# Zero matmuls and full columns in the first stage of a fused Fourier mixer and MLP, an earlier input load, and one weight conversion moved

## The chip, the cores and the metric

The kernel runs on one core of a Trainium2 chip. The metric is device time in microseconds (us) of one execution; lower is better. All kernels here keep the reference's outputs; every run told below was correct. A run is called fast when the chip was in its normal state; all runs here are fast but one, a single execution whose state can't be told (e8), which is marked. Where a profile is read, times count from the first instruction of that execution.

## The reference, cut to what matters

A Fourier filter over 8 images of 3008 x 256, then a two-layer MLP on all 24064 rows. The two weight matrices reach the kernel as 64-bit floats, which it converts itself.

```python
def _attn_ref(x, filt_r, filt_i):
    X = np.fft.rfft(x, axis=1)
    Y = X * (filt_r + 1j * filt_i)[None, :, :]
    return np.fft.irfft(Y, n=x.shape[1], axis=1).astype(np.float32)

def _moe_ref(x, w_in, w_out):        # x: (24064, 256), w_in: (256, 2048), w_out: (2048, 256)
    h = x @ w_in
    g = h * np.clip(h + 3.0, 0.0, 6.0) / 6.0
    return (g @ w_out).astype(np.float32)
```

## The kernel before

The first image has to be transformed before anything can run in the MLP, so the kernel begins with a serial stretch. It loads the first image (`x0_load`), sends it through the first stage of its transform (`a0_unit`, eight units of 8 matmuls each), multiplies by the filter (`f_unit`, VectorE), and transforms back. Then comes the first block of 512 rows in plain form (`plain_up`, `plain_down`), in eight steps, one for each 256 columns of the hidden layer. Meanwhile VectorE converts the weights: 16 pieces, seven VectorE instructions each (an eighth, `w_abs`, is on ScalarE, which the code calls `nc.scalar` and the profile ACT). Piece 2p is needed by `plain_up(p)`, piece 2p+1 by `plain_down(p)`. From the second block on the kernel uses a recursive product with fewer multiplications; that steady part is not touched.

```python
    def a0_unit(j):
        for dh in range(2):
            ps = bank(0)
            for u in range(4):
                nc.tensor.matmul(ps[:, ds(u * P, 4 * KH)], x0[0:64 + NA, j + u, ts(dh, P)],   # 96 columns
                                 st["start"][0:64 + NA, ds(P, 4 * KH)], start=True, stop=True)
            copy(dh and j not in (8, 12), ...)
# ... (cut)
    def plain_up(p):
        st["g", 0, p] = gp.tile([P, 7, 256], FP32, name="g")
        st["h"] = [psU.tile([P, 512], FP32, name=n) for n in ("al", "be")]     # one buffer each
        for i in range(2):
            for d in range(2):
                nc.tensor.matmul(st["h"][i], w_in[p][:, 2 * d + i, :], xb(0, d), start=d == 0, stop=d == 1)
            relu(i)                # ScalarE, L563
            hswish(0, p, i)        # VectorE, L568: frees al, be
# ... (cut)
        ps = psU.tile([P, 512], FP32, name="al")
        for i in range(2):
            nc.tensor.matmul(ps, zero[:, P:2 * P], zero, start=True, stop=True)
        for j, n, bits in (0, 4, 0), (4, 4, 0), (8, 8, 1), (16, 8, 1), (24, 4, 1), (28, 4, 1):
            x0_load(j, n)
            load_bits(bits)        # 64-bit weights of one piece, 512 KB
        # ... (cut)
        for j in range(0, HC, 4):
            a0_unit(j)
            convert(j == 4)        # piece 0
        # ... (cut: the first image's filter and way back)
        x_load(1, 0)               # x of the second image, first part
        load_bits(8)
        for i in 3, 4:
            w_abs(i)
        convert(4)                 # pieces 1 to 4
        # ... (cut)
        for i, s in enumerate((0, 1, 1, 2, 3, 3, 4, 4, 5, 5, 6)):
            at(s, convert_one)     # pieces 5 to 15, in step s of the plain block
        # ... (cut)
        for c in 1, 2:
            at(c, x_load, 1, c)
```

All of SyncE's loads stand in one in-order queue: a load that waits for its buffer holds up those behind it. (In the trace before, the second x load of the second image stands behind loads of weight bits and is not issued until 98.1 us.)

## Time and profile before

| before | |
|---|---|
| median of 3 runs | 2740.15 us (2732.61 to 2745.07) |
| profiled run | 2743.62 us, span 2741.8 us |
| TensorE busy | 99% of the span |
| VectorE busy | 71% |
| where the edited lines run | first 155 us |

The page gives busy time by engine and, in 40 slices of the span, the clock that TensorE was granted. An engine can read as busy and still be slow: at half clock the same matmul is twice as long (in the trace before, 0.213 us for a matmul of 128 columns, 0.108 at full clock). So for TensorE one reads the clock beside the busy time, and the time of one instruction beside both.

I use four marks, all on VectorE: the start of the first product with the filter (L389), the start of the first conversion after the first image's transform (L241), the end of the last hswish of the plain block (L568), and the start of the first sum of the new block (L544). What lies between the marks are the parts of the beginning.

### The profile page before, as it was taken

What the parts mean: (1) busy time and instruction counts of PE and PEld (TensorE: products, weight loads), DVE (VectorE), ACT (ScalarE), POOL (GpSimd) and SP (SyncE); (2) the same over time, 40 slices, a digit from 0 to 9 for tenths busy, and PEclk for the clock granted to TensorE, in tenths of its full rate; (3) what the DMA queues carried; (4) which work ended last, traced back from release to release, by engine and by line L of the source; (5) the groups of instructions that cost most, each with busy time, mean ns of one, the idle gap of its engine ahead of it and who ended that gap; (6) DMA issues with size and microseconds to landing.
All of it is one profiled execution on the core that took longest, in us unless ns stands there. A gap on an engine that the chain in (4) does not pass through costs nothing.

```text
span 2741.8 us, 47083 instructions
## 1 busy us (share of the span) xinstructions
PE 2706.2 (99%) x18100; PEld 2408.9 (88%) x18100; DVE 1955.9 (71%) x3395; ACT 1329.3 (48%) x2662; POOL 423.1 (15%) x622
## 2 busy tenths in 40 slices
PE   8899999999999999999999999999999999999998
PEld 6578888998899988999889998899988999999997
DVE  6868766777567875678756787578775777766665
ACT  3344455445554455444554445544455444544443
POOL 2423321101211012100121001210012100100000
PEclk8999999999999999999999999999999999999999
DMA  8642233221332123321233212332123321100000
GB/s 212 183 134 78 53 89 90 72 58 47 85 90 77 50 50 91 89 69 50 56 89 98 66 42 62 88 97 69 38 58 91 92 72 39 43 23 24 19 9 16
DMA packets 119645, 195.88 MB, mean 71 GB/s; under 512 B 21561, under 2 KB 82681, under 8 KB 119105
## 3 DMA queue, kind: packets, MB, share of 16 engines
q1 hardware_dynamic: 101663, 148.19, 19.1%
q0 software_dynamic: 17152, 44.23, 7.0%
q8 instruction: 143, 2.34, 0.4%
q14 instruction: 81, 0.66, 0.1%
q10 hardware_dynamic: 606, 0.46, 0.1%
HBM read 120.86 MB, written 71.93 MB: 70 GB/s over the span
## 4 chain that ended last, share of the span: by engine, by line
PE 94%; DVE 4%; DMA 1%; issue 1%; SPq 0%; ACT 0%; POOL 0%; POOLq 0%; DVEq 0%
PE po L594 42%; PE al L518 23%; PE be L518 17%; PE psn L472 4%; PE psf L372 3%; PE psf L349 2%; PE psf L419 2%; DVE s L387 1%; DVE g L568 0%; PE po L616 0%; PE po L318 0%; PE po L372 0%; PE al L605 0%; DMA xs<-in_x_dram 0%; DMA w_all<-in_x_dram 0%
## 5 line engine op out<-in xcount | busy, mean ns | idle before, releaser
L594 PEld LDWEIGHTS po<-w_all,g 128*128 128x128 f32 x10304 | 1368.2, 191 | 142.2 <-issue 38.1
L594 PE MATMUL po<-w_all,g 128*128 128x128 f32 x10304 | 1399.4, 276 | 0.8 <-DVE g L568 0.6
L568 DVE SCALAR_TENSOR_TENSOR g<-r,h 128x512 f32<-128x512 f32 x736 | 511.9, 696 | 275.4 <-ACT r L563 263.6
L563 ACT ACTIVATE r<-h,half_c 128x512 f32<-128x512 f32 x736 | 531.2, 722 | 330.6 <-DVE h L544 318.6
L518 PE MATMUL al<-xt,w_all 128*128 128x256 f32 x2208 | 660.4, 381 | 3.9 <-DVE h L549 3.4
L518 PE MATMUL be<-xn,w_all 128*128 128x256 f32 x1472 | 437.8, 379 | 0.0
L544 DVE TENSOR_TENSOR h<-be,s 128x512 f32<-128x512 f32 x368 | 254.1, 691 | 252.1 <-PE be L518 242.1
L518 PEld LDWEIGHTS al<-xt,w_all 128*128 128x128 f32 x2208 | 335.3, 192 | 6.5 <-DVE h L549 4.7
L518 PEld LDWEIGHTS be<-xn,w_all 128*128 128x128 f32 x1472 | 279.7, 190 | 37.9
L558 ACT ACTIVATE h<-al 128x256 f32<-128x256 f32 x368 | 141.3, 384 | 347.3 <-PE al L518 347.3
L549 DVE TENSOR_TENSOR h<-al,s 128x256 f32<-128x256 f32 x368 | 156.3, 425 | 164.0 <-PE al L518 162.6
L576 DVE TENSOR_TENSOR g<-g 128x512 f32<-128x512 f32 x368 | 257.2, 699 | 12.6
L539 ACT ACTIVATE s<-al 128x256 f32<-128x256 f32 x368 | 141.4, 384 | 198.3 <-PE al L518 198.3
L530 ACT ACTIVATE s<-be 128x256 f32<-128x256 f32 x368 | 141.3, 384 | 176.4 <-PE be L518 176.4
L518 PE MATMUL al<-xn,w_all 128*128 128x256 f32 x736 | 219.9, 381 | 0.5 <-ACT h L558 0.5
L518 PE MATMUL be<-xt,w_all 128*128 128x256 f32 x736 | 218.9, 379 | 0.0
L529 ACT ACTIVATE s<-al 128x256 f32<-128x256 f32 x368 | 141.3, 384 | 70.9 <-PE al L518 70.9
L361 POOL DMA_DIRECT2D z_tmp<-t x192 | 111.1, 582 | 414.0 <-ACT t L352 411.5
L575 DVE TENSOR_TENSOR g<-g 128x256 f32<-128x256 f32 x368 | 162.5, 441 | 12.6
L578 DVE TENSOR_TENSOR g<-g 128x256 f32<-128x256 f32 x368 | 161.0, 437 | 12.5
L518 PEld LDWEIGHTS be<-xt,w_all 128*128 128x128 f32 x736 | 139.8, 190 | 18.9
L650 POOL TENSOR_TENSOR o<-p,o 128x256 f32<-128x256 f32 x45 | 32.7, 727 | 793.9 <-ACT t L422 397.7
(138 smaller groups left out, 1917.9 us busy)
## 6 DMA issues: line engine op xcount, KB each, us to landing
g_tmp<-t POOLq DMA_DIRECT2D x96, 256.0 KB, 3.8
t<-g_tmp SPq DMA_DIRECT2D x188, 120.0 KB
t<-z_tmp SPq DMA_DIRECT2D x42, 512.0 KB
z_tmp<-t POOLq DMA_DIRECT2D x192, 96.0 KB, 3.2
out_dram<-o SPq DMA_DIRECT2D x321, 47.0 KB
xs<-in_x_dram SPq DMA_DIRECT2D x112, 128.0 KB
ft<-in_filt_r_dram SPq DMA_DIRECT2D x88, 128.0 KB
ft<-in_filt_i_dram SPq DMA_DIRECT2D x88, 128.0 KB
```

The costliest lines, as they stand in the source:

```text
L518: nc.tensor.matmul(ps, w_in[p][:, w, :], x, start=start, stop=stop, skip_group_check=True)
L529: nc.scalar.activation(out=s[:, 0, :], in_=al, func=AXT.Copy)
L530: nc.scalar.activation(out=s5, in_=be[:, 1, :], func=AXT.Copy)
L539: nc.scalar.activation(out=s[:, 1, :], in_=al, func=AXT.Copy)
L544: nc.vector.tensor_tensor(out=st["h"][0].rearrange("p (a n) -> p a n", a=2), in0=be, in1=s, op=ALU.add)
L549: nc.vector.tensor_tensor(out=st["h"][1][:, 256:512], in0=al, in1=s5, op=ALU.add)
L563: nc.scalar.activation(out=r, in_=st["h"][i], func=AXT.Relu, bias=half_c, scale=1.0 / 6.0)
L568: nc.vector.scalar_tensor_tensor(out=st["g", k, p][:, o:o + 2, :].rearrange("p a n -> p (a n)"), in0=st["r", i], scalar=1.0, in1=st["h"][i ...
L575: v.tensor_tensor(out=g[:, G1, :], in0=g[:, G3, :], in1=g[:, G22, :], op=ALU.add)
L576: v.tensor_tensor(out=g[:, G3:G2 + 1:2, :], in0=g[:, G3:G1 + 1, :], in1=g[:, G11:G11 + 1, :].broadcast_to([P, 2, 256]), op=ALU.subtract)
L578: v.tensor_tensor(out=g[:, G4, :], in0=g[:, G12, :], in1=g[:, G2, :], op=ALU.subtract)
L594: nc.tensor.matmul(st["po", k][bank][:, part, u, :], g[:, a, ts(u, P)], w_out[p][:, w, :], start=(p == 0 and n in OPENS and u == 0), stop= ...
```

## The change

The intent: keep TensorE's clock up while the first image is still arriving, by running matmuls on zeros in the waits and by streaming all 128 columns instead of 96 (the 32 more columns hold zeros and are not read); and shorten the way to the first hswish, by moving one conversion from ahead of the MLP into it and loading a second part of the next image's x earlier.

```diff
-                nc.tensor.matmul(ps[:, ds(u * P, 4 * KH)], x0[...], st["start"][0:64 + NA, ds(P, 4 * KH)],
+                nc.tensor.matmul(ps[:, ts(u, P)], x0[...], st["start"][0:64 + NA, ts(1, P)],
...
-        for i in range(2):
-            nc.tensor.matmul(ps, zero[:, P:2 * P], zero, start=True, stop=True)
+        def keep_warm(n):
+            for i in range(n):
+                nc.tensor.matmul(ps, zero[:, P:2 * P], zero, start=True, stop=True)
+        keep_warm(2)
...
             a0_unit(j)
+            keep_warm({4: 2, 12: 2, 20: 1}.get(j, 0))
...
-        x_load(1, 0)
-        load_bits(8)
-        for i in 3, 4:
-            w_abs(i)
-        convert(4)
+        for c in range(2):
+            x_load(1, c)
+            load_bits(7 + c)
+        w_abs(3)
+        convert(3)
...
-        for i, s in enumerate((0, 1, 1, 2, 3, 3, 4, 4, 5, 5, 6)):
+        for i, s in enumerate((0, 1, 1, 2, 2, 3, 3, 4, 4, 5, 5, 6)):
...
-        for c in 1, 2:
-            at(c, x_load, 1, c)
+        at(2, x_load, 1, 2)
```

(Cut: repeated operands, marked by "[...]".)

More of the change, by code (lines that the diff above doesn't have):

```diff
@@ L317, in a0_unit @@
             for u in range(4):
-                nc.tensor.matmul(ps[:, ds(u * P, 4 * KH)], x0[0:64 + NA, j + u, ts(dh, P)], st["start"][0:64 + NA, ds(P, 4 * KH)],
+                nc.tensor.matmul(ps[:, ts(u, P)], x0[0:64 + NA, j + u, ts(dh, P)], st["start"][0:64 + NA, ts(1, P)],
                                  start=True, stop=True)
```

## The prediction

> **What bounds the kernel now.** I read the page's engine totals first, then the chain that ended last, then windows, waits and the time-ordered listing of the first 160 us, because every edited line runs there.
>
> The page says who owns the whole span:
>
> ```profile
> PE 2706.2 (99%) x18100; PEld 2408.9 (88%) x18100; DVE 1955.9 (71%) x3395; ACT 1329.3 (48%) x2662; POOL 423.1 (15%) x622
> PEclk8999999999999999999999999999999999999999
> ```
>
> TensorE is busy 99% and at full clock, except in the first slice (68.5 us each). The steady part after about 160 us is not touched, and its work is placed by steps, so a shorter beginning moves everything after it by the same amount. The question is how many microseconds the beginning loses and how many come back.
>
> Windows of that beginning (columns: stretch, length, then PE, PEld, DVE, ACT, POOL busy with counts, granted clock, DMA share, GB/s):
>
> ```profile
> 11.39:15.17 3.78, 3.78 (x32) 3.62 (x32) 2.50 (x6) 2.56 (x3) 0.00 (x0) 1.00 1.04 234
> 17.26:29.98 12.72, 12.72 (x65) 12.59 (x65) 2.72 (x4) 3.32 (x4) 1.37 (x3) 0.55 0.91 226
> 34.57:64.20 29.63, 28.27 (x135) 17.06 (x135) 27.59 (x40) 12.53 (x22) 4.75 (x8) 0.98 0.79 225
> 83.95:149.20 65.25, 61.87 (x228) 35.98 (x228) 58.31 (x92) 23.15 (x38) 31.17 (x50) 0.93 0.67 184
> ```
>
> Row one is the third and fourth first-stage unit: 32 matmul instructions in 3.78 us, 0.118 us each. Row two is the last four units, the same work twice over, 0.199 us per instruction, at clock 0.55. "PE busy" hides this: it says 100%. Row three, the transform of the first image, has VectorE (DVE) at 93%, row four, the plain first block, at 89%. So after the first stage VectorE is the engine that sets the pace until about 149 us.
>
> The waits of TensorE in 0 to 160 us:
>
> ```profile
> PE al L605 <- DVE g L568: 7.0, 2, 5.8
> PE po L318 <- DMA w_all<-in_x_dram: 2.4, 2, 2.1
> PE psf L349 <- DMA xs<-in_x_dram: 2.2, 1, 2.2
> ```
>
> and the chain around the last of them, followed by VectorE's own idling there:
>
> ```profile
> 98.60 8.39 DMA xs<-in_x_dram
> 107.13 2.44 PE psf L349 x8
> 109.58 5.94 PE po L616 x16
> 115.51 1.72 PE al L605 x4
> ```
>
> ```profile
> DVE g L568 <- ACT r L563: 3.4, 3, 1.8
> DVE w_all L259 <- ACT s L232: 0.9, 1, 0.9
> ```
>
> Each wait of 2 us or more drops the clock. The granted clock goes to 0.50 from about 18.6 to 35.7, 80 to 86.9 and 107.3 to 114.2 us. The L616 group of 16 takes 5.94 us in the third stretch, 3.47 to 3.72 elsewhere.
>
> **What the Trainium skill says.** "TensorE: Matmul & The Clock Gate", Part 1: the array's clock is gated to half after an idle window and released after a busy one; the window is about 3.4 us and free-running. This trace agrees: the switches are 3.41 us apart or multiples of it. It does not give the threshold; here the window 15.18 to 18.59, PE busy 1.33 of 3.41 us, was enough to lose the clock. More telling, four following windows were "busy" and did not bring it back; the first to do so held the 256-column L372 matmuls.
>
> Same page, Part 2, "LDWEIGHTS": a weight load's time follows the number of weight columns, not the rows. In the trace the 96-column matmuls (0.118 us at full clock, 0.199 at half) are no faster than the 128-column transposes of L330 (8 in 36.08 to 36.62 and before: one each 0.108 us; 0.213 at half). So they are spaced by loading 128 weight columns, and a quarter of each slot streams nothing. My reading (estimate): 96/128 = 75% activity is too little to release the gate; 128 of 128 is enough. And the extra 32 columns cost nothing.
>
> "SBUF — State Buffer", "Who interferes with whom": a VectorE instruction with two SBUF inputs contends with a GpSimd one that reads SBUF. The trace fits: conversions with GpSimd sums beside them take 5.2 to 6.0 us (120.3 to 131.5), others 4.2 to 4.7.
>
> **The change, part by part.**
>
> *Zeros and full columns, first stage.* A zero matmul is two instructions of 512 columns. From transposes of 128 columns at 0.108 us, that is 0.43 us each at full clock, 0.86 us per zero matmul; at half clock the opening ones show 0.855 us per instruction. Unit pairs are 32 instructions at 0.109 = 3.5 us.
> Before: units 0 and 4 end 11.08, wait to 11.39, units 8 and 12 end 15.17, wait to 17.26 for x, then 12.72 us at half clock to 29.98.
> After: 11.1 + 1.7 (two zeros) = 12.8; + 3.5 = 16.3; + 1.7 = 18.0, past the arrival of x at 17.26; + 3.5 = 21.5; + 0.85 = 22.4; + 3.5 = 25.9. The zeros overshoot two waits (1.4 and 0.7 us): the price of the warm clock. Net 4.1 us on the path, since the last units' x, issued right behind and moved at 226 GB/s (750 KB, 3.4 us), is there by about 21 us.
> The first transposes and first L372 group then also run at full clock. Last copy 26.8, half a turn 0.5, ACT copy 0.6, four L372 instructions 0.9: VectorE's first product starts at about 29.0 instead of 34.57. So this part is worth 5.5 us. The first filter tables must be there by 28 us; they are issued 17.4 to 20.4 us and follow that x at the same rate (768 KB, 3.5 us: estimate 24.5). Later groups gain the same, since TensorE's loop (4.67 us per group) and VectorE behind it only shift.
>
> *Three conversions instead of four.* A conversion is seven VectorE instructions, 4.2 to 4.7 us. TensorE's 5.83 us wait for L568 at 83.49 falls to about 1.6 us: relu ends at 78.4 because its buffers wait for L419, ending 77.66, and conversion 3 ends at 78.1 on the old clock. The cold stretch after it disappears. But VectorE is continuous from 54 to 110 us except 0.58 us, so the conversion is moved, not removed: on VectorE's path it is worth nothing or at most 0.6 us.
>
> *x_load(1,1) ahead.* Before, it sits in SyncE's queue behind the loads of bits that wait for conversions 6 and 7, is issued at 98.1 and lands 107.1. Now it is issued at about 70, right behind the load of piece 0, and is there long before step 3. That removes the 2.2 us wait and the half-clock L616 (5.94 - 3.7 = 2.2), and with it what VectorE lost: 0.89 + 1.84 + 1.03 = 3.8 us idle.
>
> Check by VectorE's sum: hswish of step 0 can start 78.5, conversions from 79.85; twelve conversions at the observed times (4.3, 4.4, 4.2, 4.64, 4.63, 4.95, 4.6, 5.6, 5.24, 4.65, 4.67, 4.65 = 56.5) and seven hswish pairs at 1.25 (8.8) give 145.2, against 149.2 before. So 3.9 us, on the old clock, for the last two parts together, of which the x load is nearly all. Total 5.5 + 3.9 = 9.4 us.
>
> **The rivals.**
> 1. The first stage is bounded by DMA: 226 GB/s at 0.91 to 1.08 share from 5 to 50 us, so an earlier TensorE only waits for tables. Against it: no L372 or L389 group waits for a DMA in this trace, and estimated landings leave some 3 us. If it held, the first part would give 2 to 3 us: total 6, time 2734.
> 2. The clock is lost anyway, because the free-running window falls otherwise or zeros do not count. For: the page warns of the phase. Against: the opening zeros took part in the window that released the clock. Then part one turns into a loss of some 1 to 2 us from the zeros at half clock: total 2 to 3, time 2738. With full columns alone it should recover within two windows.
> 3. The plain stage is held by SyncE's in-order queue: z_store, x loads and tables for image 1 are issued back to back from 137.75 to 153, and ACT waits for them at 153.6. The load before them waits for conversion 13, VectorE's, so the queue moves with VectorE; if not, 2 to 4 us vanish: time 2733 to 2735.
> 4. The kernel before is sometimes luckier than this trace: runs of 2732.6 to 2745.1 fit a gap of 2.09 us that sometimes straddles two windows. Then the change helps the median less than the profile.
>
> **Range and chances.** The profiled run took 2743.62 us; minus 9.4 is 2734. The median before is 2740.15; minus 9.4 is 2730.8. I take 2731.5, leaning to the median. Run-to-run spread of before is 12 us, and the gain may lie between 4 and 12 us, so 2725 to 2738. Two per cent is 55 us; all idle and half-clock loss of the beginning together is under 30, so faster by 2% is 1%, slower by 2% 0.5%.
>
> **What would show each step.** First-stage units at about 0.11 us per instruction throughout, ending near 26 us; clock 1.00 from 8 to 60 us; first L389 near 29. No 5.8 us wait of L605 for L568, instead two or more of 1 to 4 us. L349 without a wait for xs; its load issued near 65 us. VectorE busy over 95% through the plain stage; the first L518 near 141 instead of 151 (150.80). I am wrong if L372 or L389 waits for a table, if the clock is 0.50 between 18 and 35, or if the steady part changes at all: that would move more than everything above.

## The result, and the profile after

The changed kernel took 2734.43 us in the median of 4 runs (2733.80 to 2735.95), beside 2741.46 us for the kernel before on the same chip (four runs with the three from above: 2732.61 to 2745.07). The ratio of the two is 0.998, with a 95% interval of 0.9955 to 1.0005, so "same" at the 2%. The interval holds 1. With e5 below, the changed kernel has eight runs of 2733.80 to 2738.80 us, and 31 of the 34 of the kernel before are above 2738.9. Ratios here are the mean time of one kernel's fast runs over that of the other's of the same rounds, so not quite the ratio of the medians. The profiled runs give spans of 2733.2 and 2741.8 us: 8.6 us apart. All outputs are right.

The page's totals and the granted clock of the kernel after:

```profile
PE 2701.7 (99%) x18110; PEld 2401.1 (88%) x18110; DVE 1954.6 (72%) x3395; ACT 1329.9 (49%) x2662; POOL 422.6 (15%) x622
PEclk9999999999999999999999999999999999999999
```

The clock's first digit went from 8 to 9; TensorE has 4.5 us less to do although ten zero instructions were added, because the same matmuls ran at full clock. Windows of the kernel after (same columns as in the prediction: stretch, length, then busy time and counts of PE, PEld, DVE, ACT, POOL, then clock, DMA share, GB/s):

```profile
17.15:25.39 8.24, 8.24 (x67) 7.57 (x66) 3.07 (x4) 3.36 (x4) 1.37 (x3) 1.00 0.88 229
28.68:57.69 29.01, 27.65 (x135) 16.64 (x134) 27.59 (x40) 12.65 (x22) 4.75 (x8) 1.00 0.95 278
73.94:139.35 65.41, 60.38 (x222) 33.53 (x221) 62.13 (x99) 24.18 (x40) 32.74 (x53) 0.95 0.66 184
```

Row one holds the last four units with a zero matmul between them: 8.24 us at clock 1.00, where before they took 12.72 us at 0.55. Row two is the first image's filter stretch, 29.01 us instead of 29.63. Row three is the plain block: VectorE is now busy 95% (62.13 of 65.41), against 89% before.

TensorE's waits for 0 to 160 us have no line for the first image's x (L318) and none for the second image's (L349) any more. A line that names the x load (`xs`) remains, L500's, and has grown from 0.4 to 1.2 us; but L500 reads `t4` and not `xs` in the code, so the name is probably that of another load. The wait for VectorE is still there, in smaller pieces (total, times, longest):

```profile
PE al L605 <- DVE g L568: 6.6, 6, 2.1
```

The last of these pieces shows in the chain that ended last:

```profile
131.89 0.61 DVE g L568
132.54 3.64 PE al L605 x4
136.18 1.72 PE be L605 x4
```

TensorE waited 2.1 us for L568, lost the clock (0.50 from 132.5 to 135.9), and took 3.64 us for what takes 1.72 at full clock. The listing in order of time has the two x loads of the second image on SyncE's queue:

```profile
62.47 1.74 SPq L288 DMA_DIRECT2D xs<-in_x_dram  x4
...
64.84 3.51 SPq L288 DMA_DIRECT2D xs<-in_x_dram  x4
```

The second used to be issued from 98.1 us on. In the marks (us; the last column is the span less the first L544):

| | first L389 | to first L241 | to end of last L568 | to first L544 | first L544 at | rest |
|---|---|---|---|---|---|---|
| before | 34.57 | 29.63 | 84.99 | 5.79 | 154.98 | 2586.9 |
| after | 28.68 | 29.01 | 81.66 | 7.03 | 146.38 | 2586.8 |
| gain | 5.89 | 0.62 | 3.33 | -1.24 | 8.60 | 0.0 |

The rest of the span is the same to 0.1 us. So all of the 8.6 us is in the beginning. VectorE is not without idling in the plain block: the first hswish now waits 1.38 us for its ReLU, as one conversion less stands ahead of it. What the table can't say is which edit earned what.

### The profile page after: what moved, and what is told of

It is laid out like the page before. It is cut to its first block, busy times and chain, and to the rows that moved or that the text cites. A ratio compares the mean times of both kernels' runs of the same rounds, so it can differ in the third digit from the quotient of the medians.

```text
span 2733.2 us, 47101 instructions
## 1 busy us (share of the span) xinstructions
PE 2701.7 (99%) x18110; PEld 2401.1 (88%) x18110; DVE 1954.6 (72%) x3395; ACT 1329.9 (49%) x2662; POOL 422.6 (15%) x622
## 4 chain that ended last, share of the span: by engine, by line
PE 94%; DVE 4%; issue 0%; ACT 0%; DMA 0%; POOL 0%; SPq 0%; POOLq 0%; DVEq 0%
PE po L594 42%; PE al L518 23%; PE be L518 17%; PE psn L472 4%; PE psf L372 2%; PE psf L349 2%; PE psf L419 2%; DVE s L387 1%; DVE g L568 1%; PE po L318 1%; PE po L372 0%; DVE y L243 0%; DVE y L254 0%; DVE g L575 0%; PE al L727 0%
## 5 line engine op out<-in xcount | busy, mean ns | idle before, releaser
L594 PEld LDWEIGHTS po<-w_all,g 128*128 128x128 f32 x10304 | 1368.2, 191 | 142.1 <-issue 38.1
L568 DVE SCALAR_TENSOR_TENSOR g<-r,h 128x512 f32<-128x512 f32 x736 | 511.6, 695 | 275.5 <-ACT r L563 263.9
L518 PE MATMUL al<-xt,w_all 128*128 128x256 f32 x2208 | 660.4, 381 | 3.9 <-DVE h L549 3.4
L518 PE MATMUL be<-xn,w_all 128*128 128x256 f32 x1472 | 437.8, 379 | 0.0
L544 DVE TENSOR_TENSOR h<-be,s 128x512 f32<-128x512 f32 x368 | 254.0, 690 | 253.5 <-PE be L518 242.3
L518 PEld LDWEIGHTS al<-xt,w_all 128*128 128x128 f32 x2208 | 335.3, 192 | 6.5 <-DVE h L549 4.7
L518 PEld LDWEIGHTS be<-xn,w_all 128*128 128x128 f32 x1472 | 279.7, 190 | 38.0
L518 PE MATMUL al<-xn,w_all 128*128 128x256 f32 x736 | 219.9, 381 | 0.5 <-ACT h L558 0.5
L518 PE MATMUL be<-xt,w_all 128*128 128x256 f32 x736 | 218.9, 379 | 0.0
L518 PEld LDWEIGHTS be<-xt,w_all 128*128 128x128 f32 x736 | 139.8, 190 | 18.9
```

Source lines behind the costliest of these rows:

```text
L518: nc.tensor.matmul(ps, w_in[p][:, w, :], x, start=start, stop=stop, skip_group_check=True)
L544: nc.vector.tensor_tensor(out=st["h"][0].rearrange("p (a n) -> p a n", a=2), in0=be, in1=s, op=ALU.add)
L568: nc.vector.scalar_tensor_tensor(out=st["g", k, p][:, o:o + 2, :].rearrange("p a n -> p (a n)"), in0=st["r", i], scalar=1.0, in1=st["h"][i ...
L594: nc.tensor.matmul(st["po", k][bank][:, part, u, :], g[:, a, ts(u, P)], w_out[p][:, w, :], start=(p == 0 and n in OPENS and u == 0), stop= ...
```

## The experiments

The theory to test: zeros and full columns together keep the clock in the first stage (5.9 us), the x load ahead gives the plain block's 3.3 us, and the moved conversion gives nothing. Rivals: one of the two first-stage edits does it all; or the moved conversion is what counts; or what is gained at the front is given back at the waits behind. Twelve runs were made (e5 repeats the changed kernel, e10 repeats e6). Medians of 4 runs (e8: one run; e12: five):

| run | kernel | median (us) | before | first L389 | to L241 | to L568 | to L544 | L544 at | rest |
|---|---|---|---|---|---|---|---|---|---|
| e1 | before + full columns | 2734.65 | 2740.70 | 27.74 | 29.01 | 84.46 | 5.80 | 147.01 | 2586.8 |
| e2 | before + zeros | 2735.30 | 2740.70 | 28.40 | 29.00 | 81.62 | 7.03 | 146.05 | 2586.8 |
| e3 | before + both | 2736.28 | 2740.70 | 29.10 | 29.01 | 82.75 | 5.80 | 146.66 | 2586.8 |
| e4 | before + x load + three conversions | 2740.30 | 2740.70 | 36.59 | 29.83 | 80.94 | 7.03 | 154.39 | 2586.8 |
| e5 | after, again | 2736.49 | 2740.81 | 29.28 | 29.01 | 81.50 | 5.80 | 145.59 | 2586.9 |
| e6 | after without zeros | 2733.07 | 2740.81 | 27.35 | 29.33 | 81.53 | 5.79 | 144.00 | 2587.0 |
| e7 | e6 with four conversions | 2735.85 | 2740.81 | 29.42 | 29.01 | 81.52 | 7.04 | 146.99 | 2586.8 |
| e8 | e1 with x of unit 16 late | 2734.06 | 2740.81 | 29.32 | 29.01 | 81.17 | 5.80 | 145.30 | 2587.0 |
| e9 | e6, last conversions later | 2731.99 | 2739.91 | 29.52 | 29.01 | 77.85 | 7.03 | 143.41 | 2586.8 |
| e10 | e6, again | 2735.31 | 2739.91 | 27.92 | 29.26 | 81.81 | 7.03 | 146.02 | 2586.8 |
| e11 | e9, tables later | 2738.86 | 2739.91 | 29.27 | 29.01 | 77.82 | 7.03 | 143.13 | 2594.1 |
| e12 | e9, one zero matmul | 2730.61 | 2741.59 | 27.53 | 29.02 | 79.52 | 7.03 | 143.10 | 2586.8 |

In e9, e11 and e12 the last conversion stands behind the last L568, so it is in the fourth part, not in the third. No clock window is lost at the end there (the last one, in all three, at 113 to 117 us): their 7.03 us are TensorE's own work behind the last L570, which is what VectorE's L568 is in these kernels.

**e1, full columns alone.**

```diff
-                nc.tensor.matmul(ps[:, ds(u * P, 4 * KH)], x0[...], st["start"][0:64 + NA, ds(P, 4 * KH)],
+                nc.tensor.matmul(ps[:, ts(u, P)], x0[...], st["start"][0:64 + NA, ts(1, P)],
```

> Kernel before with the full columns alone, no zero matmuls. Marks: start of the first L389 product (before 34.57, after 28.68 us) and of the first L544 sum (154.98 and 146.38). My theory: the 2.09 us wait for x still loses the clock in most executions, but with 128 of 128 columns the first busy windows give it back (one or two windows of 3.41 us at half clock instead of five), so the first L389 starts at 29.5 to 31.5 and the first L544 gains 3 to 5 us on before. Rival A (full columns are all that matters): clock 1.00 throughout, L389 at 28 to 29. Rival B (full columns are worthless): clock 0.50 for about 17 us, L389 at 34 to 35.

Measured: 2734.65 us (2734.51 to 2735.63), ratio 0.9978 (0.9963 to 0.9993), first L389 at 27.74. Rival A is right in this trace: the clock was 1.00 from 6.8 to 64.9 us, with no zeros at all. TensorE's part of the listing:

```profile
6.47 3.91 PE L318 MATMUL po<-p,w_all 111*128 111x128 f32 x32
11.78 3.81 PE L318 MATMUL po<-p,w_all 111*128 111x128 f32 x32 [1.40 <-DMA w_all<-in_x_dram]
17.07 7.38 PE L318 MATMUL po<-p,w_all 111*128 111x128 f32 x64 [1.48 <-DMA w_all<-in_x_dram]
```

The main expectation, a lost clock and L389 at 29.5 to 31.5, failed here; e7, e9, e10 and e11, with the same first stage, did lose the clock. The first L544 came 8.0 us earlier, expected were 3 to 5. The waits for x are still there (1.40 and 1.48 us, in brackets), the last 64 instructions take 7.38 us, and the first product is nearly 1 us earlier than in the changed kernel. And 3.81 us for 32 instructions of 128 columns is what 32 of 96 columns took before (3.78): the columns are free.

**e2, zeros alone.**

```diff
+        keep_warm(2)          # in place of the two opening zero matmuls
             a0_unit(j)
+            keep_warm({4: 2, 12: 2, 20: 1}.get(j, 0))
```

> Kernel before with the zero matmuls alone, 96 columns as before. My theory: 96 columns were only too little to win a lost clock back; if no wait loses it, it is kept: clock 1.00 from about 8 us, first L389 at 28.5 to 29.2, and the gain of the whole first-stage part (5.5 to 6.5 us at the first L544, less what the rest of the way takes). Rival (75% activity also loses the clock, or cannot win it at the start): half clock for 3.4 us or more in 8 to 28 us and L389 at 30 or later.

Measured: 2735.30 us (2734.63 to 2735.72), ratio 0.9980 (0.9965 to 0.9995), first L389 at 28.40, clock 1.00 from 5.9 to 74.2 us. As the theory said: 96 columns don't lose the clock where no wait does. The first L544 came 8.9 us earlier, more than the 5.5 to 6.5 expected: x was in time at L349 here, for a reason that is taken up below.

**e3, both.** The edits of e1 and e2.

> Kernel before with zeros and full columns, the rest as before. My theory: first L389 at 28.7 as in the changed kernel, last product of VectorE in the first image's transform 6.5 us earlier, and first L544 5.5 to 6.5 us earlier than in before (148.5 to 149.5), as the VectorE-bound stretch only shifts. Rival (what is gained is given back at the waits later, on SyncE's queue or on the copies of x): first L544 at 151 or later.

Measured: 2736.28 us (2735.28 to 2737.02), ratio 0.9983 (0.9968 to 0.9998), first L389 at 29.10, first L544 at 146.66. The front's gain is not given back; the first L544 is even 2 us earlier than expected, as L349 waited 1.1 us for x instead of 2.2. But both together are not better than either: the two edits do the same thing twice, and the zeros cost TensorE time once the clock is safe (L389 at 29.10 against 27.74 in e1). e1 and e3 were run on the same chip, and every run of e1 was at or under 2735.63, three of the four of e3 over it.

**e4, the plain part alone.** The last three hunks of the change, the first stage as before.

> Kernel before with the x load ahead and three conversions ahead, first stage as before. My theory: first L389 at about 34.6 (or 28 to 29 where the execution keeps the clock by luck), the last L568 of the plain block 3 to 4 us nearer to the first L389 than in before (114.6 us from start to end there), first L544 2 to 3.5 us earlier than in before. e3 and e4 together should make the 8.6 us of the whole change within 1.5 us. Rival (the two parts need each other): e4 gains under 1 us.

Measured: 2740.30 us (2738.88 to 2742.98), ratio 0.9996 (0.9980 to 1.0013). From first L389 to the end of L568 it is 110.77 us, 3.85 less than before's 114.62, as expected. But the first L544 came only 0.6 us earlier, because this execution's first stage was 2 us slower than that of before's profile, and a clock window was lost at the end; 2 to 3.5 us were expected. In the times the part is not distinguishable from nothing. e4's loss of the clock shows what a window costs and how long it lasts. Three windows of 3.41 us in a row (columns as above):

```profile
14.20:17.61 3.41, 1.57 (x15) 1.41 (x13) 3.31 (x7) 2.42 (x3) 0.00 (x0) 1.00 0.97 192
17.61:21.03 3.42, 2.97 (x14) 3.00 (x15) 0.49 (x1) 0.82 (x1) 1.35 (x3) 0.50 1.00 218
21.03:24.44 3.41, 3.41 (x18) 3.41 (x18) 0.81 (x1) 0.82 (x1) 0.00 (x0) 0.50 0.77 207
```

TensorE is busy 1.57 of 3.41 us in the first (46%), is at half clock in the next, and stays there through windows that read as 100% busy, for 20.5 us in all (17.6 to 38.1), as before does for 17.1. The window that released it held 256-column matmuls (L372) in both.

**e5, the changed kernel again,** no edit.

> The changed kernel once more, beside the others of this call. What is open after e1 to e4: full columns alone took 6.0 us off the median, zeros alone 5.4, both 4.4, and the plain part alone 0.4. So the parts don't add. Expected: 6 to 7 us under before (2734 to 2735), first L389 at 28.5 to 29.2, first L544 at 146 to 147.

Measured: 2736.49 us (2734.27 to 2738.80), ratio 0.9988 (0.9972 to 1.0005). Expected was 2734 to 2735: these four executions were 2 us slower and scattered more. The profile has the first L389 at 29.28 and the first L544 at 145.59, both just outside what was expected. So medians of four runs are good to about 2 us, and smaller differences should be read from the marks.

**e6, the changed kernel without the zeros.**

```diff
-            keep_warm({4: 2, 12: 2, 20: 1}.get(j, 0))
```

> The changed kernel without the zero matmuls between units (full columns, x load ahead, three conversions). Theory Z: with full columns the waits for x (1.4 to 2.1 us) no longer cost the clock, and the zeros only overshoot the arrival of x: first L389 at 27.5 to 28.2, first L544 0.5 to 1.5 us earlier than in e5, median 0.5 to 1.5 us under e5, runs as tight. Rival (the zeros are an insurance): in some executions the clock is lost in 15 to 25 us, and runs scatter by over 3 us, with a median no better than e5.

Measured: 2733.07 us (2732.74 to 2735.89), ratio 0.9978 (0.9963 to 0.9994), first L389 at 27.35, first L544 at 144.00, 1.6 earlier than in e5. Three of the four runs are within 0.6 us at a mean clock of 0.998; the fourth, 2735.89, has 0.996. So theory Z holds in the profile, and so does a part of the rival: now and then an execution loses a clock window somewhere. (e10, the same kernel, has 2735.31 us and did lose one in the first stage; so in the times e6's lead on e5 is not shown.) VectorE's list names a table at the first product, and TensorE's waits name one once (total, times, longest):

```profile
27.35 0.69 DVE L389 TENSOR_TENSOR s<-po,ft 128x512 f32<-128x512 f32 x1 [0.69 <-DMA wb<-wb_t]
PE po L372 <- DMA wb<-wb_t: 0.6, 1, 0.6
```

The first is only a name: L389 waits the same 0.69 us in e5, e10 and e12, where TensorE's L372 is named, and it follows the last unit by 3.29 or 3.30 us in all of these. The second is real, but small: the second group of L372 waits 0.60 us for its table instead of 0.25 for ACT, and the stretch to L241 is 0.3 us longer (29.33, in e10 29.26, elsewhere 29.01).

**e7, e6 with four conversions ahead.** Full columns and the x load; `convert(4)` and the old list of steps stay.

> Full columns and the x load ahead, but four conversions ahead as before. Theory: the moved conversion is worth nothing, as VectorE does the same work in either order; the x load is all of the plain part, as in e1 L349 waits 2.8 us for it and loses the clock for 6.8 us. So first L544 within 1 us of e6 and 1 to 3 us before e1's (147.01), median within 1 us of e6. Rival (the conversion counts: without it L605 waits some 5 us for L568, loses the clock, and what follows is late): e7 is 1.5 us or more slower than e6.

Measured: 2735.85 us (2734.51 to 2736.49), ratio 0.9985 (0.9967 to 1.0003). Against e6 the median is 2.8 us slower, so by the time alone the rival wins. The marks say where: VectorE's plain stretch is 81.52 us, in e6 81.53. The moved conversion is worth nothing there, as expected. The rest came from the clock: this profiled execution lost a window in the first stage, which e6's did not (L389 2.07 us later), and one at the end (7.04 instead of 5.79). The first is no part of the edit, since e7 and e6 are the same kernel there; the second I can't attribute. Nor is the difference in time the edit's: e10, e6's kernel again, also lost a window in the first stage and one at the end, and has 2735.31. What the fourth conversion does is visible as a wait (total, times, longest):

```profile
PE al L605 <- DVE g L568: 6.9, 2, 4.8
```

One wait of 4.8 us, and the clock at half from 75.1 to 82.0. It costs nothing at L568, since VectorE is the bound there. Whether it makes a loss at the end likelier stays open.

The loss in the first stage is worth more than the run was meant for. Three windows of e7:

```profile
13.65:17.06 3.41, 1.65 (x15) 1.45 (x14) 3.31 (x7) 2.49 (x3) 0.00 (x0) 1.00 0.99 196
17.07:20.48 3.41, 3.36 (x16) 3.39 (x17) 0.21 (x1) 0.82 (x1) 1.36 (x3) 0.51 1.02 222
20.48:23.89 3.41, 3.41 (x32) 3.41 (x32) 1.67 (x2) 1.25 (x2) 0.00 (x0) 0.99 0.84 252
```

TensorE busy 1.65 of 3.41 us (48%) lost the clock, and one window of full columns brought it back: 16 or 17 instructions in the slow window, 32 in the next. With 96 columns, three windows that held nothing else and read as 100% busy didn't, in e4 and in before alike. e9, e10 and e11, all with full columns, lost the clock in the first stage as well, and each had it back after exactly one window (18.4 to 21.8, 13.2 to 16.6, 17.9 to 21.3 us). In the first stage these kernels differ from before and e4 in the columns alone, so four traces against two show that the columns are the cause. A further sign is in e1, where 94-column matmuls (L500) fill 2.75 of the 3.41 us from 64.85 us on: this window reads as 100% busy at half clock, and the next is at half clock too. In e12 a window with 2.15 us of them did bring the clock back; how full is full enough was not measured.

**e8, the x of unit 16 late,** one look, with full columns.

```diff
-        for j, n, bits in (0, 4, 0), (4, 4, 0), (8, 8, 1), (16, 8, 1), (24, 4, 1), (28, 4, 1):
+        for j, n, bits in (0, 4, 0), (4, 4, 0), (8, 8, 2), (16, 8, 2), (24, 4, 2), (28, 4, 2):
```

> Before with full columns, but the second load of weight bits (512 KB, about 2.3 us at 226 GB/s) put ahead of the x of unit 16, so that the wait before unit 16 is 3.7 us or more and the clock is lost for certain. It measures the recovery. Theory: with 128 of 128 columns streaming, the first full window gives the clock back: half clock for one or two windows (3.4 to 6.8 us). Rival (full columns only helped by keeping the clock, they do not win it back sooner): half clock for four or five windows, until the L372 products, as in before and e4 (17.1 and 20.5 us).

Measured: 2734.06 us, one run, state unknown. The expectation failed: the wait was 3.3 us and the clock was not lost, so e8 measured no recovery (e7 did). The reason is in the windows (their place is known from the later switches, which are multiples of 3.41 us away):

```profile
13.55:16.96 3.41, 1.77 (x16) 1.58 (x15) 3.31 (x7) 2.59 (x3) 0.00 (x0) 1.00 0.96 196
16.96:20.38 3.42, 1.75 (x15) 1.78 (x16) 0.14 (x1) 0.58 (x1) 1.36 (x3) 1.00 0.98 218
```

The wait straddles two windows, and TensorE is busy 51 to 52% in both. A wait of 3.3 us was survived by luck of its place; 1.8 us in e7, nearly all in one window, was not.

**e9, e10, e11: later conversions.** VectorE bounds the plain block, but at its end TensorE still has about 6 us of work behind the last L568. e9 exchanges the last pieces so that TensorE can start `plain_up(7)` earlier, and converts piece 15 after the last L568, since only `plain_down(7)` in the next block needs it.

```diff
+    PART = {13: 14, 14: 13}          # used in w_part and for the sums
...
-        for i, s in enumerate((0, 1, 1, 2, 2, 3, 3, 4, 4, 5, 5, 6)):
+        for i, s in enumerate((0, 1, 1, 2, 2, 3, 3, 4, 4, 5, 6, 7)):
```

> An attempt to beat both: e6 (no zeros) with each of the last conversions as late as its reader allows. Pieces 13 and 14 change places (the first product of step 7 needs 14, the second product of piece 6 needs 13), and piece 15 is converted after the last hswish pair of the plain block. Theory: after VectorE's last piece of plain work, before and e1 to e8 all needed 5.8 us to the first L544 (7.03 with a lost clock window), as TensorE had product 7, piece of x, down 6 and the new block's first products behind it. If two conversions stand after TensorE's start of product 7 instead of one, TensorE works beside them, and the first L544 comes 2 to 5 us earlier than in e6 (139 to 142), median 2 to 4.5 us under e10. Rival (SyncE's queue holds it: tables for image 1 in front of the z stores, ACT's L352 waits): gain under 1 us, L352 or L539 waiting instead.

Measured: 2731.99 us (2730.84 to 2733.14), ratio 0.9969 (0.9954 to 0.9984). Its profile lost a window in the first stage (L389 at 29.52), yet its first L544 is at 143.41. That is later than the 139 to 142 expected, as L389 came 2.2 us later than in e6. From L389 to L544 it needs 113.89 us, e6 116.65.

e10 is e6 once more, as a base.

> e6 once more as the base for e9 and e11, and as a second sample of its clock: 2732.5 to 2734 where the clock is kept before 30 us, 2735 to 2737 where one window is lost. First L544 at 143.5 to 147.

Measured: 2735.31 us (2732.91 to 2737.59), ratio 0.9982 (0.9965 to 0.9998), first L389 at 27.92, first L544 at 146.02. The runs go roughly with the mean clock: 2732.91 at 0.998, 2735.97 at 0.997, 2734.64 and 2737.59 at 0.996.

e11 asks for the second image's tables two steps later, behind the z stores.

```diff
-                s = b_at[2 * (c - FB) + 1] + 1 if c >= FB else a_at[-1 if n > 1 else 3] + 1
+                s = b_at[2 * (c - FB) + 1] + 1 if c >= FB else a_at[-1 if n > 1 else 5] + 1
```

> e9 with the tables of image 1 asked for two steps later, behind the z stores in SyncE's queue. If SyncE's queue holds e9, this is 1 to 3 us faster than e9 (first L544 at 138 to 141); if it doesn't, the two agree within 1 us. If the tables then come too late for image 1's first product, a new wait for wb or ft shows after 170 us and the rest of the span (2586.9 us from first L544 to the end in all runs so far) grows.

Measured: 2738.86 us (2738.05 to 2739.65), ratio 0.9994 (0.9979 to 1.0009). First L544 at 143.13, as in e9, so SyncE's queue does not hold e9 there. But the rest of the span grew from 2586.8 to 2594.1 us, with one new wait in 150 to 200 us:

```profile
PE psf L374 <- DMA t<-z_tmp: 4.5, 1, 4.5
```

The second image's first product waits 4.5 us (this kernel's L374 is the L372 of before), and the clock is then at half for 6.8 us. The early table loads look idle for 20 us but keep the queue free for what must come later.

**e12, e9 with one zero matmul,** in the longest wait only.

```diff
             a0_unit(j)
+            keep_warm({12: 1}.get(j, 0))
```

> e9 with one zero matmul (0.86 us) in the longest wait only, after unit 12: it ends at about 16 us, before x comes at 16.7 to 17.3, so it costs no time and leaves a wait of at most 1.3 us. Theory: full columns and a short wait keep the clock in every execution, first L389 at 27.3 to 28.2 (e9: 29.52 with one lost window), first L544 at 141 to 142.5, median 0.5 to 2 us under e9's 2731.99, and a spread under 2 us. Rival (one zero is too little or comes at the wrong place): L389 at 29 or later in the profile and a median within 0.5 us of e9.

Measured, in 5 runs: 2730.61 us (2729.88 to 2731.70), ratio 0.9960 (0.9947 to 0.9974), first L389 at 27.53, first L544 at 143.10 against 141 to 142.5 expected. TensorE's list (this kernel's L320 is L318, and L729 are the zeros):

```profile
11.24 3.81 PE L320 MATMUL po<-p,w_all 111*128 111x128 f32 x32 [0.70 <-DMA w_all<-in_x_dram]
14.89 1.02 PE L729 MATMUL al<-r 128*128 128x512 f32 x2
16.86 7.38 PE L320 MATMUL po<-p,w_all 111*128 111x128 f32 x64 [0.94 <-DMA w_all<-in_x_dram]
```

The zeros end before x comes; 0.94 us of wait is left, and no time is lost in the first stage. That one profile kept the clock there does not show that every execution does. It has the lowest median here: 11.0 us under before's of its call, where the changed kernel is 7.0 and 4.3 under in its two. Against e9, the intervals of the ratios overlap, so that this zero gains time is not shown. The first L544 is later than expected because a window was lost after the first stage (65.2 to 68.6 us), and the first hswish waited 3.04 us for its ReLU, 1.53 in e9:

```profile
73.48 0.69 DVE L570 SCALAR_TENSOR_TENSOR g<-r,al 128x512 f32<-128x512 f32 x1 [3.04 <-ACT r L565]
```

VectorE's list at the end of the plain block shows what is left:

```profile
133.79 0.68 DVE L570 SCALAR_TENSOR_TENSOR g<-r,al 128x512 f32<-128x512 f32 x1
135.38 0.69 DVE L570 SCALAR_TENSOR_TENSOR g<-r,be 128x512 f32<-128x512 f32 x1 [0.91 <-ACT r L565]
...
139.73 0.69 DVE L261 SCALAR_TENSOR_TENSOR w_all<-s,y 128x512 f32<-128x512 f32 x1
143.10 0.69 DVE L546 TENSOR_TENSOR h<-be,s 128x512 f32<-128x512 f32 x1 [2.68 <-ACT s L541]
```

L570 is the last hswish, L261 the end of piece 15, now inside what used to be an idle stretch, L546 the first sum of the new block. VectorE still waits 2.68 us for it, now for TensorE and ACT.

## Why the prediction was right or wrong

**The time.** 2734.43 us lies in the range of 2725 to 2738, 2.9 us over the predicted 2731.5. The predicted gain was 9.4 us, the traces show 8.6 and the medians 7.0. That difference is rival 4 of the prediction: the kernel before is sometimes luckier than its profile. In all, 34 runs of it were taken; three took 2732.1 to 2733.0 us, the others 2739.0 to 2745.1. The mean clock is known for two of the three, 0.997, where the others of those calls have 0.993 or 0.994. They probably kept the clock in the first stage; that is inferred, as none of them was traced.

**First stage: right in size, incomplete in cause, and partly luck.** Units were to end near 26 us and L389 to start at 29.0; they ended at 25.4 and it started at 28.68. The clock was to be 1.00 from 8 to 60 us; it was, from 6.2 to 112. The sum took unit pairs as 3.5 us and two zeros as 1.7; they took 3.64 to 3.73 and 1.74 to 1.86, 0.7 us more in all. Luck made up for it: the clock was granted at 6.2 us in this execution, at 8.35 in before's, and the first two units ended 1.2 us earlier. In e5, where it came at 8.1, the units end at 25.99 and L389 is at 29.28, so 0.6 of the 5.9 us is the place of the clock window. "The extra 32 columns cost nothing" holds (3.81 against 3.78 us). "75% activity is too little to release the gate" held in before and e4, and full columns got it back in one window in e7, e9, e10 and e11. What failed is the step that called the zeros' overshoot "the price of the warm clock". It need not be paid in every execution: e1 has no zeros between units and an L389 at 27.74, e6 at 27.35. But full columns alone kept the clock in three of seven traces only (e1, e6, e8), zeros in all five that have them. With both (28.68, 29.10 and 29.28 in after, e3 and e5) L389 is 0.9 to 1.9 us later than with full columns that keep their clock (e1, e6; in e8 x came late), and about as late as with full columns that lose a window before unit 16 (29.3 to 29.5 in e7, e9 and e11). So these five zero matmuls are an insurance that costs about what one lost window does; e12's single one cost nothing.

**"Each wait of 2 us or more drops the clock": wrong as a rule.** The wait's place counts. Waits of 3.3 us (e8) and 1.4 to 1.5 us (e1) kept it, waits of 1.8 (e7), 1.7 (e9) and 1.6 us (e10) lost it. In the windows measured in the first stage, 36 to 52% busy lost it (e11 1.23 of 3.41 us, before 1.33, e4 1.57, e7 1.65, e9 1.67, e10 1.77), and 51 and 52% kept it in e8: the border is at about half, and no sharper than that in these runs. Later in the traces it blurs: windows of 42% (e8, from 129.6 us) and 43% (e5, from 110.5) kept the clock, and one of 66% lost it (e3, from 97.9), in which TensorE ran matmuls of 94 columns or 47 rows.

**Three conversions: right.** Worth nothing on VectorE's path; e6 and e7 agree to 0.01 us. What the fourth conversion no longer fills shows as the wait for the first ReLU (1.38 us in after, where the prediction's sum had 0.4; 1.54 in e6; none in e7, where L568 waits 1.11 us later instead). TensorE's wait of 5.83 us became six of at most 2.1, as foreseen.

**x load ahead: mechanism right, but it is not always needed.** Foreseen were 3.8 us of VectorE's idling, the plain stretch gained 3.33. But e2 and e8, without this edit, have 81.62 and 81.17 us too: x came in time there. The wait for it was 2.2 us in before, 2.8 in e1, 1.1 in e3, none in e2 and e8. In these traces it goes roughly with the time that SyncE took for the eight issues of the two loads: 8.8, 8.6, 7.3, 5.6 and 6.0 us. So this edit takes away a risk of up to 3.5 us rather than a fixed cost. In the traces the first-stage edits alone brought the first L544 forward by 8.0, 8.9 and 8.3 us (e1, e2, e3), the whole change by 8.6, and in the times e4 is no faster than before: a gain in time from the two later edits is not shown. Why the issues' time varies stays open.

**The term that was missing.** My sum ended at VectorE's last hswish: predicted to fall by 9.4 us, it fell by 9.8 (149.19 to 139.35). The first L518, foreseen near 141, came at 142.41. Behind the last hswish 1.24 us were lost again, as the last of the new waits of TensorE for VectorE cost a clock window (5.79 us became 7.03; as the lost window also put off the last hswish, its whole price at L544 is 1.7 us, 13.9 from the L568 that released L605 against 12.2 in e5). I had foreseen waits of 1 to 4 us and the clock's sensitivity, but not put the two together. It is not there in every execution: e5, the same kernel, has 5.80. Rival 3, SyncE's queue, was not what took it: e9 and e11 agree to 0.3 us at the first L544.

**Tables.** I would be wrong "if L372 or L389 waits for a table". In the changed kernel's trace the first L389 waits 0.7 us, and a DMA of tables is named; but the same wait stands there in e5 with TensorE named, so nothing was lost to tables. In e6 the second L372 group did wait for one, which cost 0.3 us. Rival 1 is thus a bound close by, but it took nothing from this change.

**Conversions beside GpSimd.** The prediction's line between 5.2 to 6.0 and 4.2 to 4.7 us is drawn too sharply. In the trace before, a conversion takes 4.26 us with no GpSimd sum beside it, 4.72 with 1.9 to 2.1 us of sums, 5.92 (at 106.1 us, which the prediction left out) with 3.0 and 6.07 with 5.4. That agrees with the page it cites; no run tests it.

## What to carry to other kernels

A matmul stream that reads as 100% busy can be stuck at half clock when it fills only part of each slot; look at the time of one instruction and the clock, and fill the columns first, since that cost nothing here (3.81 against 3.78 us for 32 instructions, whose weight loads fill 3.62 us). Filler matmuls are the second means: only in the waits that need them and so short that they end before the data comes. And an edit that removes a wait has to be followed to the next engine that sets the pace: here a conversion moved along VectorE's path changed TensorE's largest wait and no time, while moving one behind VectorE's last needed product, where TensorE had work to do beside it, gained 2.8 us from the first product to the first sum (e9 against e6; in the times, e9's median is 3.3 us under e10's).

## What the Trainium skill lacked or had wrong

- "TensorE: Matmul & The Clock Gate", Part 1, gives an idle window of about 3.4 us as what lowers the clock, and advises against TensorE gaps over some 3 us. Here far less is enough: windows with TensorE busy 39% (before), 46% (e4), 48% (e7) and even 52% (e10) lost it, by waits of 2.1, 2.3, 1.8 and 1.6 us. Windows with 51 and 52% (e8, a wait of 3.3 us across two of them) kept it, so in the first stage about half busy is the border; later, 42 and 43% kept it and 66% lost it once each. The window's length and its free running agree with all traces.
- The same page does not say that a busy-looking stream of ordinary matmuls can fail to raise the clock because each fills only part of its slot. At 96 of 128 columns per weight load, three windows of 3.41 us, all 100% busy, left it at half in before and in e4; at 128 columns it came back after one window in four of four cases.
- The same page's note on zero operands is about the current limiter; it does not say whether matmuls on zeros keep the clock up. They do: in e2, where they are the only edit, the clock was 1.00 through the whole first stage (from 5.9 us on).
- No page says how a profile shows the clock before its first record. Here the views print 1.00 from the first instruction on, while the opening zero matmuls take 0.855 us per instruction of 512 columns, twice the 0.43 us of those after 10 us in e5. The kept traces have no clock record before 5.7 to 8.4 us, and the views count time without one as full clock; it is no wrong record.
